# A list-scheduled attention and MLP kernel on one core: new order biases and planner costs, no instruction changed

## The chip, the cores and the metric

The kernel runs on one core of a Trainium2 chip. The metric is the device time of one execution in microseconds (us). The engines are TensorE (PE, with its weight loads shown as PEld), VectorE (DVE), ScalarE (ACT), GpSimd (POOL) and SyncE (SP). POOL and SP also issue the DMA transfers, each from its own queue, in order.

## The reference

```python
# attention: q, k, v are (8 batches, 8 heads, 576 positions, 64)
scores = q @ k.T / sqrt(64)
rel = i - j
mask_plain = (rel >= 0) & (rel < 32)                      # heads 0 to 3
mask_dil = (rel >= 0) & (rel < 128) & (rel % 4 == 0)      # heads 4 to 7
attn = softmax(where(mask, scores, -1e9)) @ v
x = attn.transpose(0, 2, 1, 3).reshape(4608, 512)
# MLP with a gated activation
h = x @ w_in                                              # 512 -> 2048
g = h * sigmoid(beta * h)
out = g @ w_out                                           # 2048 -> 512
```

## The kernel before, in words

The 4608 tokens are cut into 9 tiles of 512, and the work has two strands that are woven together. One is the MLP of a tile: for each of 16 blocks of the 2048 hidden columns `slot_h` issues four matmuls of 512 columns (L888), a tanh on ACT (L897) and the gate on DVE (L902); then `block_cols` multiplies with w_out, 16 matmuls of 512 columns for each 128 tokens (L923), evacuates on ACT (L938) or DVE (L940), and SP stores the rows (L943). The other is the attention of a batch (0 to 7), 576 tokens each. While the MLP of tile t is on PE, attention t + 1 is to be computed.

One attention has these parts, named by the lines that show in the profile:

- Loads. For batches 0 to 2 POOL loads q, k and v in bfloat16 straight into staging tiles (L395), and PE transposes q and k (L470 for the dilated heads, L480 for the plain ones), with copies out of PSUM at L244. From batch 3 on, POOL's loads write q and k as bfloat16 into scratch in DRAM (`s`), and SP reads them back with DMA transposes (L461) into dk and dq (dilated) and kT and qT (plain). Such a list of loads starts with a tiny POOL copy, `pace` (L1002). For batch 3 it waits for a gate of tile 1, and from batch 4 on for the transposed attention output xT of batch b - 2, both halves of it.
- V. vd is the dilated heads' V, vt the tail of it and vp the plain heads' V. vp has overlapping windows, so 32 rows are copied once more after its load: the halo copy, at L244 as `vp<-vp`, on DVE or POOL as the planner chooses. dkt is a copy of the last dilated keys, by `mixed` (L244), and qt the last queries.
- Scores on PE (L684 dilated, L653 its tail, L748 plain for batches 0 to 2 and L712 plain from 3 on, 24 at once), the exponential on ACT (L620), the mask on DVE or POOL (L624, tiles ptd, ptt and pt), the product with V on PE (L789 dilated, L774 tail, L805 plain), and the normalisation on DVE (L639, L640, into xdm, xdt and xsp).
- The way back. For batches 0 and 1 PE transposes the outputs (L842, L857, L827) into xT. From batch 2 on SP stores them to scratch `x` (L507, L515, L520) and reads them back by DMA transposes into xT (L534), two for a batch: xT0 and xT1.

Nothing of this order is written out by hand. Every piece is recorded as an `Op` in the class `Plan`: with the engines that it may run on and a cost in ns for each, the ops that it depends on, a due value `vt` and a bias, looked up in the table `NUDGE` by the op's number. `Plan.run` then does a list scheduling with these costs: for each engine it takes, among the ops that can start earliest (start plus bias, within the slack `NEAR`), the one with the smallest due value. The order that comes out is the order in which each engine's instructions are emitted, and an engine works strictly in that order, waiting on semaphores. `LAP` (L52) lets the planner start the next op on ACT or DVE 105 or 80 ns before the last one ends, if that one costs over 250 ns (L149). If the planner sees PE without work for more than 170 ns (300 early on) within the first 80 us, it emits a zero matmul (`filler`, L1036, 256 columns) into the hole. So a changed cost or bias can move any instruction of any queue.

The lines where the planner's costs stand: `mixed` at L582, the mask at L625, the halo copy in `direct_vp` at L417.

```python
picks = []
for e, c in near.items():
    first = min(s + o.bias for s, o, _ in c)
    s, o, d = min((x for x in c if x[0] + x[1].bias <= first + self.NEAR[e]), key=lambda x: (x[1].vt, x[0]))
    picks.append((s, o.vt, e, o, d))
```

Of the kernel before, what the change touches and what calls it, by code (L numbers as in the profile page):

```python
# [10 lines left out]
ACT = mybir.ActivationFunctionType  # L11
# [28 lines left out]
class Plan:  # L40
# [3 lines left out]

    CAPS = {"h": 3, "p": 4, "o": 2, "z": 4, "a": 8, "s": 5, "w": 6}
    SWITCH = 95
    NUDGE = {4: 900, 12: 900, 97: 400, 99: 150, 165: -900, 173: 150, 241: 60, 247: 400, 250: 900,
        268: -60, 285: 900, 299: -400, 309: 60, 312: -150, 362: 150, 405: 900, 424: -150, 496: 60,
        522: -900, 539: 150, 541: 900, 547: 150, 576: -400, 583: -400, 647: -150, 667: 900,
        675: -400, 717: -900, 796: -900, 808: 400}  # L50
    LAT = {"PE": 210, "ACT": 45, "DVE": 45, "POOL": 60, "SP": 0}
    LAP = {"PE": 0, "ACT": 105, "DVE": 80, "POOL": 0, "SP": 0}  # L52
    NEAR = {"PE": 40, "ACT": 60, "DVE": 60, "POOL": 60, "SP": 0}

    def __init__(self, banks):
# [2 lines left out]
    def op(self, engs, fn, deps=(), vt=0.0, acquire=None, group=None, dma=0, lat=None, halves=False, sbuf=False):  # L58
        acquire = acquire if acquire is None or isinstance(acquire, list) else [acquire]
        o = Op(engs, fn, deps, vt, acquire, group or acquire, dma, lat, halves, sbuf)  # L60
        o.bias = self.NUDGE.get(len(self.ops), 0)
        self.ops.append(o)
        return o

    def run(self, filler=None, filler_until=0.0):
        free = {"PE": 1100.0, "ACT": 1300.0, "DVE": 1000.0, "POOL": 1300.0, "SP": 1300.0}
# [22 lines left out]
        def bank_at(gs, start):  # L89
            kind, more = gs[0].kind, len(gs)  # L90
            n = [x.release for x in ends if x.kind == kind and x.release > start]
            n_open = sum(1 for x in held.values() if x.kind == kind)
            if n_open + more > self.CAPS[kind]:
                return None
            over = n_open + len(n) - self.CAPS[kind] + more
            if over > 0:
                start = sorted(n)[over - 1]
            open_banks = {x.bank for x in held.values()}
            times = sorted(t for b, t in bank_free.items() if b not in open_banks)
            return max(start, times[more - 1]) if len(times) >= more else None  # L100

        while n_left:
            best = None
            near = {}
            for o in avail:
                base = o.ready
                at = {e: max([free[e], base] + [t for x, t in o.group.read.items() if x != e]
                             if o.group is not None and e != "PE" else [free[e], base]) for e, d in o.engs}
                if o.sbuf:
                    at = {e: max(t, port["DVE" if e == "POOL" else "POOL"]) for e, t in at.items()}  # L110
                fin = min(at[e] + d for e, d in o.engs)
                for e, d in o.engs:
                    start = at[e]
                    if start + d > fin + 100:
                        continue
                    if o.dma and len(lanes[e]) >= 8:
                        start = max(start, lanes[e][-8])
                    if o.acquire is not None:
                        start = bank_at(o.acquire, start)
                        if start is None:  # L120
                            continue
                    near.setdefault(e, []).append((start, o, d))
# [5 lines that stand above are left out]
            assert picks, "no work can start"  # L128
            s, _, e, o, d = min(picks, key=lambda x: (x[0], x[1]))
            if filler is not None and s <= filler_until and free["PE"] + (300 if free["PE"] < COLD else 170) < s:  # L130
                now = free["PE"]
                open_banks = {x.bank for x in held.values()}
                spare = [b for b, t in bank_free.items() if b not in open_banks and t <= now]
                if spare:
                    filler(max(spare, key=lambda b: -bank_free[b]))
                free["PE"] = now + (225 if now < COLD else 115)
                halves = False
                continue
            for g in o.acquire or ():
                open_banks = {x.bank for x in held.values()}  # L140
                g.bank = min((b for b, t in bank_free.items() if b not in open_banks and t <= s + 1e-6),
                             key=lambda b: -bank_free[b])
                held[id(g)] = g
                g.left = len(g.users)
            o.fn(e)
            if e == "PE" and o.halves != halves:
                halves = o.halves
                d += self.SWITCH
            free[e] = s + d - (self.LAP[e] if d > 250 else 0)  # L149
            if o.sbuf:  # L150
                port[e] = s + d
            o.start, o.end = s, s + d + self.LAT[e]
            if o.group is not None and e != "PE":
                o.group.read[e] = o.end
            if o.dma:
                at = max(dma_free[e], s + d + 900)
                other = max(dma_free.values()) - at
                dma_free[e] = at + o.dma + max(0.0, min(o.dma, other))
                o.end = dma_free[e] + (o.lat or 1100)
                lanes[e].append(o.end)  # L160
            avail.remove(o)
            n_left -= 1
            for x in o.next:
                x.waits -= 1
                x.ready = max(x.ready, o.end)
                if not x.waits:
                    avail.append(x)
            for g in list(held.values()):
                if o in g.users:
                    g.left -= 1  # L170
                    if not g.left:
                        del held[id(g)]
                        g.release = max(u.end for u in g.users)
                        bank_free[g.bank] = g.release
                        ends.append(g)
            ends[:] = [g for g in ends if g.release > s - 5000]
# [9 lines left out]
def kernel(  # L186
# [49 lines left out]
    plan = Plan(range(8))  # L236
# [6 lines left out]
    def copy(e, out, in_):  # L243
        (nc.scalar.copy if e == "ACT" else E[e].tensor_copy)(out=out, in_=in_)  # L244
# [293 lines left out]
    def attention(b, ld, names, vts):  # L538
# [40 lines left out]

        def mixed(e):  # L580
            copy(e, dkt[kv], dk[kv][:, :, :, CT - KTL:].rearrange("p r h k -> p h k r"))
        o = plan.op([("DVE", 360), ("POOL", 550), ("ACT", 500)], mixed,  # L582
                    (steps["KD0"] + steps["KD1"] if b < DIRECT else ready["D"][0:1]) + war(("dkt", kv)), vt_of["T"] - .01, sbuf=True)
        used(("dk", kv, 0), o)
        used(("dk", kv, 1), o)
# [2 lines left out]
        for c in range(2):  # L588
            def padded(e, c=c):
# [3 lines left out]
            o = plan.op([("DVE", 250), ("POOL", 500), ("ACT", 290)], padded,  # L593
                        (steps["QD0"] + steps["QD1"] if b < DIRECT else ready["D"][1:]) + [fill1] + war(("qt", kv)),
                        vt_of["T"] - .01, sbuf=True)
# [10 lines left out]
        def spread(e):  # L606
            copy(e, vd[kv][:, :, :, 0:D], vd16_of[b])
        o = plan.op([("POOL", 1100), ("DVE", 620), ("ACT", 1030)], spread,
                    [ld["vd"][0], (fill3, fill4)[kv]] + war(("vd", kv)), vt, sbuf=True)
# [7 lines left out]
        def exp_and_mask(key, sop, g, vt, n, sc, w, m, tiles):  # L617

            def expo(e):
                nc.scalar.activation(out=w(), in_=sc(), func=ACT.Exp, scale=SCALE)  # L620
            ex = plan.op([act(n)], expo, [sop, fill2] + war(*tiles), vt - .005, group=g)
            if b >= ADDED or key == ("T",):
                def mask(e):
                    E[e].tensor_tensor(out=w(), in0=w(), in1=m(), op=ALU.mult)  # L624
                ex = plan.op([("POOL", 170 + 2.2 * n), ("DVE", 160 + .53 * n)], mask,  # L625
                             [ex] + [mask_tail if key == ("T",) else mask_ops["D" if key[0] in (2, 3) else "n"]],
                             vt, sbuf=True)
            wrote(*tiles)
            sdone[key] = ex
# [324 lines left out]
    for n, (c0, c1) in enumerate(((0, 512), (512, 1024), (1024, 2048))):  # L954
        o = load("POOL", (w_in_bf[:, :, c0:c1], moe_w_in[:, c0:c1].rearrange("(c p) d -> p c d", p=P)),
                 [], -7.3 + .01 * n, (c1 - c0) * 2, .41)
        for fb in range(c0 // P, c1 // P):
            w_in_ld[fb] = o
    for n in range(2):
        o = load("POOL", (w_out_bf[:, 8 * n:8 * n + 8, :],  # L960
                          moe_w_out[n * 8 * P:(n + 1) * 8 * P, :].rearrange("(c p) d -> p c d", p=P)),
                 [], -7.2 + .01 * n, 2048, .41)
# [107 lines left out]
```

## Time and profile before

| what | value |
| --- | --- |
| runs | 307.88, 305.89 and 303.32 us |
| median | 305.89 us |
| the profiled execution | 307.88 us, its span 306.1 us |
| PE busy in the span | 297.0 us, 97% |
| DVE, ACT, POOL busy | 190.8, 169.1 and 83.9 us |
| zero matmuls (L1036) | 61, 10.1 us busy |
| mean clock of PE | 1.0 in every slice but two (0.8) |
| DMA | 41.98 MB moved, mean 137 GB/s |

All times below are counted from the start of the span. A timeline row has the start, the length, the engine, the line, the operation with its tiles, and in brackets the idle time of the engine just before it and what ended that. Busy times of PE contain matmuls that overlap, so they can add up to more than the stretch that they fill.

### The profile page before, as it was taken

The numbers are of one execution on the slowest core, as the hardware profiler recorded it, in microseconds if no ns is written. First come the engines' busy times: TensorE is split into PE (matmuls) and PEld (weight loads), VectorE is DVE, ScalarE is ACT, GpSimd is POOL, SyncE is SP. The second block draws the span as 40 slices with busy tenths as digits, with TensorE's granted clock in tenths as the row PEclk, the third lists the DMA queues.
The fourth block names the chain that finished last, engine by engine and source line by source line (L and its number), as shares of the span: only waits on it lengthen the run. The fifth ranks groups of instructions, "written<-read, shape, count | busy, mean of one in ns | idle before, by whom it ended". The sixth has DMA issues, their size and how long they took to land.

```text
span 306.1 us, 6067 instructions
## 1 busy us (share of the span) xinstructions
PE 297.0 (97%) x2338; PEld 150.2 (49%) x2338; DVE 190.8 (62%) x429; ACT 169.1 (55%) x306; POOL 83.9 (27%) x121
## 2 busy tenths in 40 slices
PE   7999999999799999999999999999999999999996
PEld 5765455554354444544545454445444444444444
DVE  4668887799647846974678778656862534334300
ACT  3878932787334747754476657454744544455411
POOL 8997333681018005600632009100000000000000
PEclk9999999999889999999999999999999999999999
DMA  7999999699949999999699969995025000100122
GB/s 164 181 208 202 206 178 231 82 144 166 207 118 177 169 162 185 195 144 238 129 184 155 181 153 138 178 219 152 36 75 112 34 34 35 36 34 34 41 98 69
DMA packets 111248, 41.98 MB, mean 137 GB/s; under 512 B 87620, under 2 KB 104596, under 8 KB 111220
## 3 DMA queue, kind: packets, MB, share of 16 engines
q0 software_dynamic: 60336, 18.58, 58.8%
q1 hardware_dynamic: 50740, 22.95, 37.4%
q8 instruction: 18, 0.29, 0.4%
q14 instruction: 10, 0.08, 0.1%
q10 hardware_dynamic: 144, 0.07, 0.1%
HBM read 37.76 MB, written 18.87 MB: 185 GB/s over the span
## 4 chain that ended last, share of the span: by engine, by line
PE 83%; DMA 8%; DVE 4%; POOL 2%; ACT 1%; issue 1%; ACTq 0%; DVEq 0%; POOLq 0%
PE bank L923 38%; PE bank L888 36%; DMA vp<-in_v_dram 6%; DMA st<-in_q_dram 2%; PE bank L805 2%; DVE pt L624 1%; PE bank L1036 1%; PE bank L789 1%; PE bank L712 1%; POOL s L395 1%; DVE xdm L640 1%; PE bank L684 1%; PE bank L470 1%; PE bank L774 1%; DVE g L902 1%
## 5 line engine op out<-in xcount | busy, mean ns | idle before, releaser
L923 PE MATMUL bank<-w_out_bf,g 128*128 128x512 bf16 (+2 forms) x608 | 142.4, 370 | 0.0
L897 ACT ACTIVATE tnh<-bank,beta_half 128x512 bf16<-128x512 f32 x144 | 98.5, 689 | 74.8 <-PE bank L888 71.2
L902 DVE SCALAR_TENSOR_TENSOR g<-tnh,bank 128x512 bf16<-128x512 bf16 x144 | 97.5, 685 | 67.7 <-ACT tnh L897 66.9
L888 PE MATMUL bank<-xT,w_in_bf 128*128 128x512 bf16 (+2 forms) x584 | 138.7, 376 | 0.0
L888 PEld LDWEIGHTS <-w_in_bf 128*128 128x128 bf16 x584 | 55.3, 98 | 61.5 <-issue 1.1
L923 PEld LDWEIGHTS <-g 128*128 128x128 bf16 x608 | 55.4, 98 | 57.4 <-issue 1.0
L938 ACT ACTIVATE osb<-bank 128x512 f32<-128x512 f32 (+1 forms) x30 | 17.2, 576 | 28.2 <-PE bank L923 28.1
L620 ACT ACTIVATE pt<-bank 128x384 bf16<-128x384 f32 (+1 forms) x54 | 20.2, 469 | 7.6 <-PE bank L712 6.4
L620 ACT ACTIVATE ptd<-bank 128x512 bf16<-128x512 f32 x32 | 17.0, 605 | 6.9 <-PE bank L684 6.8
L624 DVE TENSOR_TENSOR pt<-pt,mask_n 128x384 bf16<-128x384 bf16 (+1 forms) x42 | 16.4, 415 | 5.4 <-ACT pt L620 5.1
L640 DVE TENSOR_TENSOR xsp<-bank,rcp 96x384 bf16<-96x384 f32 x32 | 17.7, 554 | 1.1
L1002 POOL COPY pace<-xT 1x2 bf16<-1x2 bf16 x4 | 0.7, 176 | 57.8 <-DMA xT<-x 57.8
L395 POOL DMA_DIRECT2D vp<-in_v_dram x9 | 15.2, 1695 | 0.4 <-DVE rcp L639 0.4
L639 DVE RECIPROCAL rcp<-bank 128x4 f32<-128x4 f32 (+2 forms) x72 | 12.8, 177 | 3.6 <-PE bank L789 2.9
L940 DVE TENSOR_SCALAR osb<-bank 128x512 f32<-128x512 f32 (+1 forms) x8 | 5.3, 658 | 14.8 <-PE bank L923 14.7
L395 POOL DMA_DIRECT2D vt<-in_v_dram x16 | 14.4, 1032 | 0.0
L640 DVE TENSOR_TENSOR xdm<-bank,rcp 128x256 bf16<-128x256 f32 x32 | 13.6, 425 | 1.1
L395 POOL DMA_DIRECT2D s<-in_q_dram x10 | 13.5, 1349 | 0.0
L624 DVE TENSOR_TENSOR ptd<-ptd,mask_d 128x512 bf16<-128x512 bf16 x27 | 10.9, 421 | 3.0 <-ACT ptd L620 2.4
L805 PEld LDWEIGHTS <-pt 128*128 128x128 bf16 x192 | 9.1, 97 | 6.0 <-DVE pt L624 1.1
L395 POOL DMA_DIRECT2D s<-in_k_dram x10 | 11.0, 1103 | 1.5 <-issue 1.1
L1036 PE MATMUL bank<-zero 128*128 128x256 bf16 x61 | 10.1, 303 | 1.1 <-DVE warm L303 1.1
(112 smaller groups left out, 179.6 us busy)
## 6 DMA issues: line engine op xcount, KB each, us to landing
out_dram<-osb SPq DMA_DIRECT2D x35, 256.0 KB, 2.6
s<-in_k_dram POOLq DMA_DIRECT2D x10, 288.0 KB, 5.9
s<-in_q_dram POOLq DMA_DIRECT2D x10, 288.0 KB, 8.8
w_out_bf<-in_moe_w_out_dram POOLq DMA_DIRECT2D x2, 1024.0 KB, 16.5
vp<-in_v_dram POOLq DMA_DIRECT2D x7, 288.0 KB, 17.5
st<-in_q_dram POOLq DMA_DIRECT2D x6, 288.0 KB, 11.1
x<-xsp SPq DMA_DIRECT2D x12, 144.0 KB, 6.9
st<-in_k_dram POOLq DMA_DIRECT2D x5, 288.0 KB, 13.4
```

The lines of the kernel that those rows point to most:

```text
L395: {"POOL": nc.gpsimd, "SP": nc.sync}[queue].dma_start(out=out, in_=in_)
L620: nc.scalar.activation(out=w(), in_=sc(), func=ACT.Exp, scale=SCALE)
L624: E[e].tensor_tensor(out=w(), in0=w(), in1=m(), op=ALU.mult)
L639: nc.vector.reciprocal(out=r, in_=p[..., D])
L640: nc.vector.tensor_tensor(out=dst, in0=p[..., 0:D], in1=r.unsqueeze(len(p.shape) - 1).to_broadcast(list(p.shape[:-1]) + [D]), op=ALU.mult)
L805: nc.tensor.matmul(pv[:, a, h2, :], lhsT=lhs, rhs=vp[kv][:, (2 * x + h2) * NI + 3 * j + a, 0:D + 1], start=True, stop=True)
L888: nc.tensor.matmul(bank(g)[:, a:z], lhsT=w_in_bf[:, kt, fb * P:(fb + 1) * P], rhs=xT[:, kt, xo + a:xo + z], start=(i == 0 and kt == kts[0] ...
L897: nc.scalar.activation(out=th[:, 0:n], in_=bank(g)[:, 0:n], func=ACT.Tanh, scale=beta_half[:, fb:fb + 1])
L902: nc.vector.scalar_tensor_tensor(out=g_t[t % 2][:, fb, c0:c0 + n], in0=th[:, 0:n], scalar=1.0, in1=bank(g)[:, 0:n], op0=ALU.add, op1=ALU.mult)
L923: nc.tensor.matmul(bank(g)[:, lo:hi], lhsT=g_t[t % 2][:, fb, tb * P:(tb + 1) * P], rhs=w_out_bf[:, fb, lo:hi], start=(fb == 0), stop=(fb = ...
L938: nc.scalar.mul(out=ob[:, lo:hi], in_=bank(g)[:, lo:hi], mul=0.5)
L1036: nc.tensor.matmul(BANKS[b][:, 0:256], lhsT=zero[:, 0:P], rhs=zero[:], start=True, stop=True)
```

## The change

Four edits, all in what the planner knows; the code that issues instructions stays.

1. `NUDGE`, the table of biases by op number, is replaced by another one.
2. `LAP` is removed: an engine counts as free only when the cost of its last op has passed.
3. The planner's cost for `mixed` on DVE goes from 360 to 450 ns.
4. The planner's cost for a mask on DVE goes from 160 + 0.53 n to 160 + 0.8 n ns, n being the elements of a row.

```diff
-    NUDGE = {4: 900, 12: 900, 97: 400, 99: 150, 165: -900, 173: 150, 241: 60, 247: 400, 250: 900,
-        268: -60, 285: 900, 299: -400, 309: 60, 312: -150, 362: 150, 405: 900, 424: -150, 496: 60,
-        522: -900, 539: 150, 541: 900, 547: 150, 576: -400, 583: -400, 647: -150, 667: 900,
-        675: -400, 717: -900, 796: -900, 808: 400}
+    NUDGE = {9: -400, 35: 400, 78: -150, 90: 150, 103: -900, 156: -900, 164: -60, 191: -60, 208: 150,
+        220: 900, 247: -400, 251: 60, 266: -150, 268: -150, 270: -150, 326: 900, 376: 400,
+        397: 900, 420: 900, 432: -900, 490: 900, 525: 150, 545: 60, 554: 900, 562: -60, 571: 60,
+        574: 150, 1103: -400, 1113: 400}
     LAT = {"PE": 210, "ACT": 45, "DVE": 45, "POOL": 60, "SP": 0}
-    LAP = {"PE": 0, "ACT": 105, "DVE": 80, "POOL": 0, "SP": 0}
...
-            free[e] = s + d - (self.LAP[e] if d > 250 else 0)
+            free[e] = s + d
...
-        o = plan.op([("DVE", 360), ("POOL", 550), ("ACT", 500)], mixed,
+        o = plan.op([("DVE", 450), ("POOL", 550), ("ACT", 500)], mixed,
...
-                ex = plan.op([("POOL", 170 + 2.2 * n), ("DVE", 160 + .53 * n)], mask,
+                ex = plan.op([("POOL", 170 + 2.2 * n), ("DVE", 160 + .8 * n)], mask,
```

What comes out of the planner differs in these places (line numbers as before; the same instructions otherwise):

- Zero matmuls: 67 for 61. Between 36 and 45 us of the profile, where 17 stood, 6 stand. Eight now stand within tile 0's L888 matmuls (after 8 of a dense run), where none did.
- Attention 0: half of the dilated K transposes follow those of q; both halves of the dilated scores come together after the plain K transposes; dkt is copied by DVE, and was by ACT.
- Attention 3: vp is loaded before plain q, and was after it; its halo copy is on POOL ahead of the tail mask, and was on DVE ahead of the dilated masks. On SP's queue qT's transpose stands before the store of batch 2's first plain output, and stood after it.
- Attention 4: vd is loaded early and vp last, and vd was last. The halo copy stays on DVE ahead of the four dilated masks; the copies of vd and dkt come earlier, between gates. On SP's queue the transposes xT0 and xT1 of batch 3 follow qT, and stood before and after kT.
- Tiles 2 and 3: L888 and L923 are interleaved otherwise.
- From batch 6 on the two orders nearly agree.

## The prediction

> **What bounds the kernel now.** I read the engines' shares first, then the slices, the chain that ended last, and then only the places where TensorE (PE) isn't dense.
>
> ```profile
> PE 297.0 (97%) x2338; PEld 150.2 (49%) x2338; DVE 190.8 (62%) x429; ACT 169.1 (55%) x306; POOL 83.9 (27%) x121
> PE   7999999999799999999999999999999999999996
> PEclk9999999999889999999999999999999999999999
> DMA  7999999699949999999699969995025000100122
> PE 83%; DMA 8%; DVE 4%; POOL 2%; ACT 1%; issue 1%; ACTq 0%; DVEq 0%; POOLq 0%
> ```
>
> PE is the bound: 97% busy and 83% of the chain. One slice is thin, the eleventh (76.5 to 84.2 us), and the granted clock dips there and just after. But busy is not useful: L1036 puts zero matmuls into holes. So I priced every other PE instruction at its dense start-to-start time in this trace (216 ns for 512 columns, 29 to 30 ns for 65, 109 to 110 ns for a zero matmul) and added them up: 283.4 us of useful work, and the last matmul ends at 303.1. Hence 1.1 us pass before PE's first work, 18.6 are lost to fillers and waits, and 3.0 follow behind it. The running loss is 9.1 at 19 us (the dense w_in run begins), 9.1 at 27, 12.7 at 44.5, 13.2 at 76.7, 17.1 at 95, and 18.6 at the end. So there are three places: the prologue, 36 to 44.5, and 76.7 to 85.
>
> ```profile
> 0.00:19.30 19.30, 16.65 (x266) 11.76 (x267) 12.54 (x44) 12.68 (x29) 17.27 (x37) 1.00 1.18 179
> 36.40:44.50 8.10, 7.38 (x74) 4.27 (x71) 7.21 (x19) 4.40 (x12) 3.79 (x6) 1.00 1.79 183
> 76.70:85.20 8.50, 6.42 (x62) 3.47 (x62) 4.81 (x13) 3.48 (x7) 0.66 (x1) 0.83 1.14 187
> ```
>
> These are windows: length, then PE, PEld, DVE, ACT, POOL busy, and the granted clock (0.83 in the third). Its cause stands in the chain of waits (start, length, what):
>
> ```profile
> 61.89 18.43 DMA vp<-in_v_dram
> 80.31 0.02 issue
> 80.34 0.48 DVE vp L244
> 80.82 0.03 issue
> 80.85 0.44 DVE ptd L624
> 81.29 0.05 issue
> 81.33 0.30 PE bank L789 x4
> ```
>
> For attention 3 the plain heads' V (vp) is the last load of its list and lands at 80.3. VectorE (DVE) waits for it with the halo copy (L244), and the dilated masks (L624), which don't need vp, are queued behind that copy. PE stands 2.08 us for the first, and then runs at half clock until 84.7. The stall takes 2.2 us and the half clock 1.7 of 3.4: 3.9 together.
>
> **The change, part by part.** No instruction changes its form. Biases, two planner costs and the removed overlap only alter the order on each queue, the engine of a few copies, and the zero matmuls (61 become 67). So each moved stretch is walked.
>
> A. Prologue: the K copy dk for pair 1 comes later on DVE, and half of the K transposes come after q. By rows of this trace the first dilated scores start 0.9 us later (8.65 becomes 9.55), the first plain ones 0.7 (11.79 becomes 12.45), and the dense w_in run 0.8. I take +0.8; the bounds are -0.4 (the fewer K transposes ahead of q help) and +2.0 (two PSUM copies of 0.64 and 0.75 behind the late one fall on PE).
>
> B. Eight zero matmuls now stand inside tile 0's L888 run, which had none: 8 x 0.11 = +0.9 where PE has work waiting, 0 where it would have waited anyway. I take +0.9.
>
> C. From 36 to 45 us, 17 zero matmuls (17 x 0.11 = 1.9 us) become 6 (0.7), and the scores come earlier. Of the 3.6 us lost there 1.7 were waits; about 1.0 stays, since four DVE normalisations of 0.55 us each still pace the back transposes (L842). 3.6 becomes 1.7: -1.9. The bounds are -2.9 (only the 0.7 stays) and 0 (PE stands idle where fillers stood).
>
> ```profile
> 42.70 0.38 PE L842 MATMUL bank<-ident_b,xdm 128*128 128x128 bf16 x4 [0.66 <-DVE xdm L640]
> 42.92 0.82 PE L1036 MATMUL bank<-zero 128*128 128x256 bf16 x6
> 43.80 0.38 PE L842 MATMUL bank<-ident_b,xdm 128*128 128x128 bf16 x4
> 44.02 0.60 PE L1036 MATMUL bank<-zero 128*128 128x256 bf16 x4
> ```
>
> D. Attention 3's halo copy moves to GpSimd (POOL), and vp is loaded ahead of plain q (s_1_0). DVE then reaches the masks with nothing to wait for: -3.9 (bounds -4.0 and 0). On POOL the copy takes 1.24 us for 0.48 and the tail mask, 0.7, stands behind it. With vp landing near 75 (plain q's old place) both end near 77, and their reader L774 comes at 67.6 useful plus 14.2 lost, 81.8: PE's own work covers them. If vp landed at 80.3 all the same, they would end at 82.3, and 0.5 would show.
>
> E. What D gives meets what D's swap delays. Plain q now has vp's place in POOL's list and lands at about 80.3 instead of 74.4.
>
> ```profile
> 60.79 2.17 POOL L395 DMA_DIRECT2D s<-in_q_dram  x1
> 61.89 2.25 POOL L395 DMA_DIRECT2D vp<-in_v_dram  x1
> 75.84 3.92 SPq L461 DMA_TRANSPOSE qT<-s  x1
> 87.10 1.31 SPq L534 DMA_TRANSPOSE xT<-x  x1
> 90.70 0.18 POOL L1002 COPY pace<-xT 1x2 bf16<-1x2 bf16 x1 [11.09 <-DMA xT<-x]
> ```
>
> On SP's queue qT's transpose waits for it, and behind qT now stand two x stores and both xT transposes of attention 2 (before, qT had gone out at 75.84). PE without D's stall would reach the plain scores (L712) at 71.65 of useful work plus 18.3 - 0.2 - 3.9 of loss = 85.9; qT lands 4.8 to 6.6 us after its issue (rows of attentions 4 and 3), at 85.1 to 86.9, so this is about even. Then: stores issue at 84.6 and land 2.7 later, xT0 at 87.3, an out store, xT1 at 89.3, landing 3.6 later: 92.9 (before 90.65). PE reaches tile 2's L888 at 77.06 + 14.2 = 91.3. So +1.6; the bounds are 0 and 6.6 (qT takes the 10.5 us of dk and dq in a loaded queue, landing at 90.8: 4.9 of stall and 1.7 of half clock).
>
> F. The pace copy that starts attention 4's loads waits for this xT1, so they start 2.2 us later. Their vp is now the last in the list, and its halo copy is still on DVE, ahead of all four masks.
>
> ```profile
> 113.31 0.48 DVE L244 COPY vp<-vp 32x1280 bf16<-32x1280 bf16 x1 [2.12 <-DMA vp<-in_v_dram]
> 114.77 0.43 DVE L244 COPY vd<-st 128x1024 bf16<-128x1024 bf16 x1 [0.98 <-DMA st<-in_v_dram]
> 115.11 1.74 DVE L624 TENSOR_TENSOR ptd<-ptd,mask_d 128x512 bf16<-128x512 bf16 x4
> ```
>
> The same stall was in the trace already, but PE came to L789 only at 117.17. The last load landed 24.1 us after the pace copy here, 20.3 in attention 5, 26.5 in 6. After the change two xT transposes stand behind qT and leave this window, so I take the middle of 24.1 and 20.3, 22.2: vp at 115.1, the first mask ready 0.95 later, 116.0; PE is there at 98.85 + 15.8 = 114.7. +1.3; the bounds are 0 (20.3) and 4.9 (24.1: 3.2 and half clock).
>
> G. Likewise attention 5: attention 3's xT1 now stands behind qT of 4 and lands at about 121 (before 117.85), and it paces 5's loads. dq, 21.6 us after its pace, lands at 142.6, and PE wants the scores at 124.35 + 17.0 = 141.4.
>
> ```profile
> 143.86 0.62 PE L684 MATMUL bank<-dq,dk 64*128 64x128 bf16 x16
> ```
>
> Before, dq landed at 139.6, 4.3 us ahead of this row; that slack is all that PE can gain here. +1.0 (bounds 0 and 3.0). From attention 6 on the orders nearly agree, and dq (166.8) has 6 us in hand: 0.
>
> Sum: 0.8 + 0.9 - 1.9 - 3.9 + 1.6 + 1.3 + 1.0 = -0.2. Against the profiled execution, 307.9 (span 306.1 and 1.8 around it), that is **307.7**. The profiled execution is 2.0 above the median of 305.9, possibly by the very stall that D takes out, so I don't take those 2 us off as well.
>
> [...] The stall of 2.08 us was followed by 3.41 us at half clock. [...]
>
> **The rivals.**
>
> R1, slower: attention 4's halo copy becomes the stall that 3's was. If the list takes 26.5 us (row of attention 6), vp lands at 92.9 + 26.5 = 119.4, the first mask is ready at 120.3, and PE has waited since 114.7: 5.6 and 1.7 of half clock instead of F's 1.3, and then nothing in G: 307.7 - 1.3 - 1.0 + 7.3 = 312.7. For it: in attentions 3, 4 and 6 the last load took 24 to 26.5 us. Against: 5 and 7 took 20. It decides once the list takes over 23.0 us, for then the hole passes the 2.1 us that cost clock.
>
> R2, the full gain: plain q lands in its old time because the list moves as a whole, and E, F and G are 0: 307.7 - 3.9 = 303.8. For it: dk, dq and kT wait for other loads, and qT's issue was bound by SP's queue. Against: the last in the list landed 5.9 us behind the one before it.
>
> R3, the early part is worse: A at +2.0 and C at 0 make 307.7 + 1.2 + 1.9 = 310.8. For it: DVE is busy 7.21 of 8.10 us in C's window, and a reordering takes nothing from it. Against: 11 fillers fewer.
>
> **How the numbers follow.** Forecast 0.42, R2 0.17, R3 0.16, R1 0.25. A measurement of this kernel tells about 2% from no change (runs spread from 303.3 to 307.9), so faster means below 299.8 and slower above 312.0. The forecast is within; R2 passes below with C's and A's good bounds (0.07 of its 0.17), R3 above with 0.05 of its 0.16, R1 with 0.18 of its 0.25: faster 0.07, within 0.70, slower 0.23. Range: from R2 with half of C's good bound, 302.0, to R1 with half of A's bad one, 313.5. The forecast's own range is 305 to 310.
>
> **What would show it.** D: L789 of attention 3 starts without a wait and the clock stays 1.0 around 80 us. E: s_1_0 lands near 80 and the pace copy near 93. F: an idle time before L789 near 115 ended by a mask behind the halo copy. G: an idle time before L684 near 142. C: loss of some 1.7 us between 36 and 45. If plain q lands at 75, E to G fall, and R2 holds; if PE isn't idle before L789 at attention 4 but the end is above 310, R3 does.

## The result and the profile after

| | kernel before | changed kernel |
| --- | --- | --- |
| median of 20 runs | 305.26 us | 303.00 us |
| shortest and longest | 303.32, 307.88 | 302.69, 303.53 |
| ratio, 95% interval | | 0.993 (0.9917 to 0.9944) |
| profiled execution | 307.88, span 306.1 | 302.73, span 301.0 |

The change makes the kernel 0.7% faster, and the interval leaves out 1; the forecast said 307.7, on the other side of the median. The ratios leave out runs that are over 1.5% longer than the kernel's fastest one, while medians are of all runs, so a ratio can differ from that of the two medians. Two things strike the eye beside that. The profiled execution of before, from which the forecast was worked out, is the longest of its 20, and the runs of the changed kernel lie within 0.8 us of each other where those of before spread over 4.6.

The page of the changed kernel (its line numbers are one lower than before's):

```profile
PE 295.5 (98%) x2344; PEld 150.4 (50%) x2344; DVE 187.5 (62%) x424; ACT 172.2 (57%) x311; POOL 83.9 (28%) x121
PEclk9999999999999999999999999999999999999999
PE 94%; DVE 2%; ACT 1%; POOL 1%; issue 1%; POOLq 0%; ACTq 0%
```

No slice has a lowered clock, and the chain that ended last is 94% PE, with no DMA in it (before: 83%, and 8% DMA). The windows that answer to those shown of before (PE, PEld, DVE, ACT, POOL busy, then the granted clock, the busy share of the DMA engines and GB/s):

```profile
36.40:44.50 8.10, 7.83 (x73) 4.04 (x71) 6.20 (x19) 5.61 (x14) 2.42 (x4) 1.00 1.84 181
76.70:85.20 8.50, 8.50 (x84) 4.44 (x82) 6.73 (x19) 4.24 (x9) 0.70 (x2) 1.00 0.86 198
```

The third place is dense. In the first of the two, DVE is busy 6.20 us instead of 7.21: that second difference turned out to matter.

To see where time was won I took PE's own work at its dense start-to-start times again, and read when each execution has done the same share of it. The orders differ, so a row is good to about half a us. `b_again` is the kernel before once more, in another execution:

| share of PE's work | before, us | b_again, us | changed, us | changed less b_again |
| --- | --- | --- | --- | --- |
| 3.0% | 21.05 | 20.88 | 20.89 | 0.0 |
| 4.5% | 24.92 | 24.74 | 25.80 | +1.1 |
| 10.4% | 47.04 | 46.85 | 46.01 | -0.8 |
| 20.4% | 77.03 | 76.83 | 76.37 | -0.5 |
| 24.1% | 91.96 | 88.35 | 87.85 | -0.5 |
| 38.9% | 133.57 | 130.39 | 129.30 | -1.1 |
| 53.8% | 176.24 | 172.66 | 171.15 | -1.5 |
| last matmul's end | 303.09 | 299.50 | 297.94 | -1.6 |

Against the execution that I had, 3.5 us come from the stall near 81 us (the rows of 20.4 and 24.1%). Against that of b_again nothing comes from there. The medians differ by 2.3 us, these two executions only by 1.5: b_again's was the shortest of its 12 runs, so the rest of the gain presumably lies in waits that it did not have.

### The profile page after: what moved, and what is told of

It is laid out like the page before. It is cut to its first block, busy times and chain, and to the rows that moved or that the text cites. A ratio compares the mean times of both kernels' runs of the same rounds, so it can differ in the third digit from the quotient of the medians.

```text
span 301.0 us, 6071 instructions
## 1 busy us (share of the span) xinstructions
PE 295.5 (98%) x2344; PEld 150.4 (50%) x2344; DVE 187.5 (62%) x424; ACT 172.2 (57%) x311; POOL 83.9 (28%) x121
## 4 chain that ended last, share of the span: by engine, by line
PE 94%; DVE 2%; ACT 1%; POOL 1%; issue 1%; POOLq 0%; ACTq 0%
PE bank L922 41%; PE bank L887 40%; PE bank L804 2%; PE bank L1035 2%; PE bank L683 1%; PE bank L788 1%; PE bank L711 1%; PE bank L469 1%; PE bank L747 1%; PE bank L479 1%; ACT ptd L619 1%; PE bank L773 1%; DVE xdm L639 1%; PE bank L673 1%; DVE ptd L623 1%
## 5 line engine op out<-in xcount | busy, mean ns | idle before, releaser
L922 PE MATMUL bank<-w_out_bf,g 128*128 128x512 bf16 (+2 forms) x608 | 140.0, 368 | 0.0
L887 PE MATMUL bank<-xT,w_in_bf 128*128 128x512 bf16 (+1 forms) x584 | 137.0, 376 | 0.0
L922 PEld LDWEIGHTS <-g 128*128 128x128 bf16 x608 | 54.5, 98 | 55.7
L937 ACT ACTIVATE osb<-bank 128x512 f32<-128x512 f32 (+1 forms) x35 | 20.6, 589 | 31.3 <-PE bank L922 30.7
L623 DVE TENSOR_TENSOR pt<-pt,mask_n 128x384 bf16<-128x384 bf16 (+1 forms) x41 | 14.8, 391 | 5.7 <-ACT pt L619 5.5
L623 DVE TENSOR_TENSOR ptd<-ptd,mask_d 128x512 bf16<-128x512 bf16 x27 | 12.0, 465 | 3.6 <-ACT ptd L619 3.0
L394 POOL DMA_DIRECT2D vt<-in_v_dram x16 | 13.3, 993 | 0.0
L1035 PE MATMUL bank<-zero 128*128 128x256 bf16 x67 | 11.6, 310 | 1.3 <-DVE warm L302 1.1
L804 PE MATMUL bank<-vp,pt 128*128 128x65 bf16 x192 | 9.8, 193 | 0.0
```

The source lines that it names most:

```text
L394: {"POOL": nc.gpsimd, "SP": nc.sync}[queue].dma_start(out=out, in_=in_)
L804: nc.tensor.matmul(pv[:, a, h2, :], lhsT=lhs, rhs=vp[kv][:, (2 * x + h2) * NI + 3 * j + a, 0:D + 1], start=True, stop=True)
L887: nc.tensor.matmul(bank(g)[:, a:z], lhsT=w_in_bf[:, kt, fb * P:(fb + 1) * P], rhs=xT[:, kt, xo + a:xo + z], start=(i == 0 and kt == kts[0] ...
L922: nc.tensor.matmul(bank(g)[:, lo:hi], lhsT=g_t[t % 2][:, fb, tb * P:(tb + 1) * P], rhs=w_out_bf[:, fb, lo:hi], start=(fb == 0), stop=(fb = ...
L937: nc.scalar.mul(out=ob[:, lo:hi], in_=bank(g)[:, lo:hi], mul=0.5)
L1035: nc.tensor.matmul(BANKS[b][:, 0:256], lhsT=zero[:, 0:P], rhs=zero[:], start=True, stop=True)
```

## The experiments

To move one instruction and nothing else, these kernels keep the planner's list (`seq`), move single entries of it, and issue the result; line numbers shift by up to some ten, by one in b_again. `at(n)` is the place of op n in the list. Names with b_ start from the kernel before, names with a_ from the changed one. `n` is the op's number: 531 is attention 3's halo copy, 530 its vp load, 525 its plain q load, 585 the second transpose of its output (xT1), 664 attention 4's kT transpose.

```python
def move(n, ahead_of, e=None):
    o, was = seq.pop(at(n))
    seq.insert(at(ahead_of), (o, e or was))
```

All ratios are to the kernel before, timed on the same chip in the same rounds; its median there lay between 304.8 and 305.6. There were four such groups of rounds, on three chips, so medians of different groups compare only to within those 0.8 us.

| kernel | median, us | shortest, longest | ratio, 95% interval |
| --- | --- | --- | --- |
| b_again | 305.60 | 304.27, 307.73 | 1.0013 (0.9984 to 1.0042) |
| b_halo | 305.19 | 303.19, 308.57 | 1.0004 (0.9975 to 1.0033) |
| b_vp | 305.32 | 303.90, 307.89 | 1.0010 (0.9977 to 1.0044) |
| b_vp_halo | 304.95 | 303.38, 308.92 | 0.9986 (0.9961 to 1.0012) |
| b_xt | 304.22 | 302.88, 309.17 | 0.9982 (0.9954 to 1.0011) |
| b_halo_xt | 304.23 | 303.10, 305.86 | 0.9974 (0.9952 to 0.9997) |
| b_nofill17 | 304.69 | 303.69, 306.33 | 0.9986 (0.9957 to 1.0015) |
| b_mask | 304.34 | 302.63, 309.16 | 0.9965 (0.9933 to 0.9998) |
| b_all3 | 303.56 | 302.36, 306.73 | 0.9962 (0.9930 to 0.9995) |
| oldbias_newcost | 303.45 | 302.18, 306.61 | 0.9952 (0.9917 to 0.9987) |
| newbias_oldcost | 312.44 | 311.08, 313.62 | 1.0238 (1.0198 to 1.0278) |
| a_undo3 | 302.87 | 302.52, 304.25 | 0.9923 (0.9891 to 0.9956) |
| a_nofill8 | 302.75 | 302.48, 302.95 | 0.9919 (0.9891 to 0.9948) |
| a_mask | 302.22 | 301.73, 303.64 | 0.9917 (0.9886 to 0.9948) |
| a_mask_nofill8 | 301.79 | 301.37, 302.92 | 0.9886 (0.9849 to 0.9923) |
| a_best | 301.67 | 301.35, 302.14 | 0.9878 (0.9843 to 0.9914) |

### The stall of attention 3

b_again changes nothing that is issued.

> The kernel before once more, nothing changed. Its profiled execution was the longest of 20 (307.88 us, median 305.26), so a second profile shows what a usual execution looks like. If the stall of attention 3 is what varies, this profile has a shorter idle time before L789 near 81 us (under 2 us), and no half clock behind it, and the span is shorter by as much, about 303.5 us. If the stall is the same (2.1 us and 3.4 us at half clock), the spread of the runs comes from elsewhere. Ratio to before 1.000.

Its profiled execution took 304.27 us. vp landed at 77.75, not 80.3, and PE did not wait for the masks at all; the clock stayed 1.0. So the 2.08 us and the half clock belong to the long execution. That a usual one lacks them is less sure, since this was the shortest run of its 12; but the profiles of b_nofill17 (304.45, near its median), b_xt and b_mask, which leave vp and the halo copy as they were, show no wait for these masks either.

b_halo:

```diff
+ move(531, 547, 'POOL')    # the halo copy, ahead of the tail mask
```

> The kernel before with one copy moved: attention 3's halo copy goes from DVE (ahead of the dilated masks) to POOL (ahead of the tail mask). Loads as before. Theory of the stall: the idle time before L789 near 81 goes, vp still lands near 80, the copy on POOL ends near 81.6 and the tail mask at 82.3, before L774 needs it or 0.5 us late; the median falls from 305.3 by 2 to 3 us, to 302.3 to 303.3. Rival, the early part: the gain of the changed kernel comes from fewer zero matmuls between 36 and 45 us, and a usual execution hardly has the stall: within 0.5 us of before.

Nothing: 1.0004, runs still up to 308.6. The interval leaves room for a gain of 0.8 us at most, not for the 2 to 3 that were expected. The stall as the gain falls, for the median at least, and so far the rival "early part" stands.

b_vp and b_vp_halo:

```diff
+ move(530, 525)            # vp ahead of plain q
+ move(531, 547, 'POOL')    # b_vp_halo only
```

> The kernel before with one load moved: attention 3's vp is loaded ahead of plain q; the halo copy stays on DVE. Theory of the stall: vp lands at 73 to 75, so the copy is over long before the masks, and the stall goes; plain q lands near 77 and qT near 81, before L712 (about 85): 302.3 to 303.3. Rival, the delay that the forecast charged: plain q lands near 80, qT near 86, the second transpose of attention 2's output near 93, and the pace copy behind it; 304.5 to 306.

> The kernel before with both moves: vp ahead of plain q, the halo copy on POOL. Theory of the stall: no more than either alone, 302.3 to 303.3, since one is enough. Rival, the two add up: vp first takes the copy's wait, POOL takes its 0.5 us from DVE; 0.5 us or more below the better of the two.

Neither differs from before. The profiles are worth more than the times. In b_vp's, a long execution of 307.76, plain q landed at 80.40 (vp at 75.23), qT went out then, and the pace copy came at 91.33, for 80.3 and about 93 in the forecast. In b_vp_halo's, a shorter one of 303.96, they were 79.46 and 90.11 (b_again, without the swap: pace copy at 87.54). So in the order of before the swap does delay the pace copy, by some 2.6 to 3.8 us against b_again, and the median doesn't show it. And b_vp's shows the next stall, in the row of tile 3's first w_in matmuls (start, length, engine, what, and the idle time before it):

```profile
117.99 1.24 PE L898 MATMUL bank<-xT,w_in_bf 128*128 128x512 bf16 x5 [1.98 <-DMA xT<-x]
```

PE waits 1.98 us for xT1 of attention 3. b_again has the same wait with 0.39 us. The execution of the forecast does not show it, since PE was 3.9 us late there when it came to it.

### Tile 3's wait for xT1

b_xt and b_halo_xt:

```diff
+ move(585, 664)            # xT1 of attention 3 ahead of kT of attention 4, on SP
+ move(531, 547, 'POOL')    # b_halo_xt only
```

> The kernel before with two moves: attention 3's halo copy on POOL, and on SP's queue the second transpose of attention 3's output (xT1) ahead of attention 4's kT, which stood before it. New theory, two stalls in turn: in the kernel before either the masks of attention 3 wait for vp, or tile 3's first w_in matmuls wait for xT1 near 115 us (0.5 to 2.1 us in the profiles so far); mending one alone only hands its time to the other. With both mended the median falls from 305.4 to about 304.0 and the longest run stays below 305.5. Rival, the early part alone: the changed kernel's gain is the 1 us between 36 and 47 us and its narrow spread has another cause; then this stays within 0.5 us of before with runs up to 308.

> The kernel before with xT1 of attention 3 ahead of attention 4's kT on SP's queue, and nothing else. Two stalls in turn: the wait of tile 3's w_in matmuls goes, that of attention 3's masks stays and is now paid in full in each run that has it; 304.5 to 305, runs up to 308. Rival, tile 3's wait alone is what costs: 304.0, and a narrow spread.

Both medians are 304.2, and in neither profile does tile 3 wait. With both moves the longest run is 305.9; with xT1 alone it is 309.2. That fits two stalls of which now one and now the other is paid, but doesn't show it: b_all3 below has both moves too, and a run of 306.7. The interval of b_xt alone includes 1, so only the pair is shown to gain, 0.03 to 0.5%. For b_xt 304.5 or more was expected; as the medians are equal, what the halo copy adds to xT1 is not shown.

In the changed kernel SP's queue is no better in this: xT1 stands behind qT. But tile 3's first w_in matmuls come later in PE's order, behind the plain scores of attention 4, and start without a wait:

```profile
118.22 0.69 PE L711 MATMUL bank<-qT,kT 64*128 64x96 bf16 x24
118.84 1.04 PE L922 MATMUL bank<-w_out_bf,g 128*128 128x512 bf16 x4
119.72 2.75 PE L887 MATMUL bank<-xT,w_in_bf 128*128 128x512 bf16 x12
```

xT1 lands at 115.19 there, 4.5 us before it is used.

### Zero matmuls

b_nofill17 leaves out the last 17 zero matmuls of before, a_nofill8 the 8 within tile 0's w_in matmuls of the changed kernel.

> The kernel before without its last 17 zero matmuls (36 to 45 us); they compute nothing that is used. If PE had work behind them, 1.9 us less: 303.5. If they only fill waits for DVE's normalisations, the holes stay as idle time: 305.4, and the clock stays 1.0 because no hole is over 1 us.

> The changed kernel without the 8 zero matmuls within tile 0's w_in matmuls; they compute nothing that is used. As the forecast's part B has it, PE has work behind them and they cost 0.9 us: 302.1 against 303.0 for the changed kernel. Rival: what follows waits for a copy or an exponential in any case, so the 0.9 us comes back as a wait by 47 us: 303.0.

b_nofill17: no difference that can be told. Most of the holes remain, as idle time ahead of the two back transposes:

```profile
43.04 0.38 PE L851 MATMUL bank<-ident_b,xdm 128*128 128x128 bf16 x4 [1.06 <-DVE xdm L649]
...
44.14 0.38 PE L851 MATMUL bank<-ident_b,xdm 128*128 128x128 bf16 x4 [0.71 <-DVE xdm L649]
```

Between two fixed PE instructions around the place (the plain scores at 36.8 and the w_out matmul at 44.5 us of b_again) its profile takes 7.39 us, b_again's 7.72: 0.33 us, not 1.9.

a_nofill8 is 0.25 us below the changed kernel, not 0.9. The medians are of different rounds, but the profiles agree: from 21 to 60 us the same PE work takes 0.23 to 0.24 us less in each of the three kernels without these eight (a_nofill8, a_mask_nofill8, a_best). The place shows a wait for the gate on DVE instead, 0.48 us of idle time in all three. Of the 1.9 and 0.9 us of fillers 0.33 and 0.25 came back: these mostly stood where PE would wait.

### Undoing attention 3's part in the changed kernel

a_undo3:

```diff
+ move(525, 530)            # plain q ahead of vp again
+ move(531, 538, 'DVE')     # the halo copy ahead of the dilated masks again
```

> The changed kernel with attention 3 put back as before: plain q ahead of vp, the halo copy on DVE ahead of the dilated masks. All else as changed. Theory: what the changed kernel has over the one before is the later place of tile 3's w_in matmuls (slack for xT1) and the 1 us before 47 us; its list for attention 3 starts 1.5 us earlier, so vp lands near 77 and the masks (80 us) hardly wait: 303.0 to 303.6, a few runs 1 to 2 us longer. Rival, the forecast's part D: without the swap the stall of up to 3.9 us is back: 304.5 to 306 with runs up to 308.

302.87 for the changed kernel's 303.00: the swap and the copy's place, which the forecast spent most of its pages on, are worth nothing in the median that can be told. Its longest run, the profiled one of 304.25, shows a halo stall at another attention:

```profile
172.03 0.30 PE L799 MATMUL bank<-vd,ptd 128*128 128x65 bf16 x4 [1.25 <-DVE ptd L634]
```

### One half of the change without the other

newbias_oldcost takes the new bias table with the old costs and overlap; oldbias_newcost the reverse.

> One part of the change alone: the new table of biases, with the planner's old costs and overlap. The biases were numbers for ops in a plan with the new costs; theory: they don't carry over, so this is another order with its own stalls, 304 to 309, above the changed kernel. Rival, the biases are the gain: 303.0.

> The other part alone: the new costs and no overlap in the planner, with the old table of biases. Theory: as for the other half, an order of its own, 304 to 309. Rival, truer costs are the gain, with any biases: 303 to 304.

The new biases on the old costs are 2.4% slower than before, above the 304 to 309 us that were expected, and the profile shows the largest cost: the wait of tile 3 at 5.54 us, and the clock at a mean of 0.69 in the 11 us from 123 on.

```profile
129.85 2.72 PE L888 MATMUL bank<-xT,w_in_bf 128*128 128x512 bf16 x6 [5.54 <-DMA xT<-x]
```

The new costs with the old biases reach 303.45, the rival's 303 to 304, but with runs up to 306.6. By the ratio this is 0.5 of the 0.7%, with an interval that includes both 0.1 and 0.8. Its profiled execution, 305.30, shows a halo stall once more, at attention 5: PE waits 1.74 us for the first dilated mask and then runs 3.41 us at half clock. So the costs alone bring a gain, the biases alone a loss, and only both together the narrow spread.

### The masks of DVE and POOL

What was open after this: 304.2 with the two stalls mended against 303.0. The stretch from 36 to 44 us differs in DVE's busy time, and b_again shows its cause. First DVE, then POOL, the plain heads' masks of attention 1:

```profile
37.54 1.42 DVE L625 TENSOR_TENSOR pt<-pt,mask_n 128x288 bf16<-128x288 bf16 x2 [0.27 <-ACT pt L621]
...
40.41 0.95 DVE L625 TENSOR_TENSOR pt<-pt,mask_n 128x288 bf16<-128x288 bf16 x2
```

```profile
37.82 0.75 POOL L625 TENSOR_TENSOR pt<-pt,mask_n 128x288 bf16<-128x288 bf16 x1
```

The execution of the forecast has the same collision:

```profile
37.72 1.47 DVE L624 TENSOR_TENSOR pt<-pt,mask_n 128x288 bf16<-128x288 bf16 x2 [0.27 <-ACT pt L620]
38.20 0.83 POOL L624 TENSOR_TENSOR pt<-pt,mask_n 128x288 bf16<-128x288 bf16 x1
```

Two such masks take 0.52 us where DVE is alone. Beside POOL's they take 1.42, and later 0.95. Everything behind them on DVE, the four normalisations first, is 1.0 us later than without (b_mask, below), and PE's back transposes wait for these. The changed kernel has one plain mask on POOL in this stretch (at 40.23) instead of two, and no DVE mask beside it. The list of differences ahead of the prediction doesn't name this one. b_mask puts POOL's two masks on DVE:

```diff
+ move(250, 171, 'DVE')
+ move(248, 276, 'DVE')     # behind the last of the four normalisations
```

> The kernel before with two masks of attention 1's plain heads on DVE instead of POOL, one in its place and one behind the last of the four normalisations near 43 us. In most profiles of the kernel before, POOL's mask starts at 37.8 to 38.4 us beside two DVE masks, and these take 1.20 and 0.73 us for 0.30; the normalisations and the back transposes on PE come 1.1 us later. In one profile (with xT1 moved) POOL came 0.3 us later, nothing was stretched, and PE lost 1.1 us less. Theory of the collision: no stretch, PE loses 0.8 to 1.1 us less before 47 us in every execution; median 304.3 to 304.8 from 305.3, stalls behind it as before. Rival, the zero matmuls and the normalisations set that stretch anyway: no change before 47 us, 305.3.

```profile
37.73 0.61 DVE L635 TENSOR_TENSOR pt<-pt,mask_n 128x288 bf16<-128x288 bf16 x2 [0.27 <-ACT pt L631]
...
40.03 0.52 DVE L635 TENSOR_TENSOR pt<-pt,mask_n 128x288 bf16<-128x288 bf16 x2
```

DVE does two masks more and is done sooner. Between the two fixed PE instructions b_mask takes 6.71 us and b_all3 (below) 6.72. Of the executions with before's masks and fillers, five take 7.72 or 7.73 and b_halo's 7.55. b_xt's takes 6.71 too: there POOL's masks happened to come later, at 38.68 and 40.19, and stretched no DVE mask. So the collision costs 1.0 us here. At 10.4% of PE's work this execution stands at 46.04 us, the changed kernel at 46.01, b_again at 46.85: the collision is as large as the net gain of the early part. It isn't the same sum, since the changed kernel also pays 0.9 us of zero matmuls there (B below). The median falls by 0.45 us beside before's in the same rounds (0.9965, 0.9933 to 0.9998).

b_all3 is b_mask and b_halo_xt together.

> The kernel before with all three: these two masks on DVE, attention 3's halo copy on POOL, xT1 of attention 3 ahead of kT of attention 4 on SP's queue. Theory: these three are the gain of the changed kernel; 304.2 (the latter two) less 0.8: 303.2 to 303.6, no run above 305. Rival, the later place of tile 3's w_in matmuls on PE brings something that these don't: 304 or more.

303.56, at the upper end of what was expected, and beside before's 304.79 in the same rounds: 0.4 of the change's 0.7% is rebuilt from three moves, in a kernel that has none of the change. The interval (0.9930 to 0.9995) reaches from the whole gain to hardly any, so what the rest is stays open. Two of the 12 runs, 305.8 and 306.7, are above the 305 that I expected as the longest. The profile, of a run of 304.07, has a wait of 0.54 us at 79.8: two dilated masks of 0.42 us took 1.44 on DVE beside POOL's halo copy, and 0.88 beside its tail mask. So the moved halo copy makes a collision of its own.

The changed kernel has such a collision too, at 61 us: DVE, then POOL, then PE.

```profile
61.39 1.55 DVE L623 TENSOR_TENSOR ptd<-ptd,mask_d 128x512 bf16<-128x512 bf16 x1 [0.55 <-ACT ptd L619]
62.86 1.23 DVE L623 TENSOR_TENSOR ptt<-ptt,mask_t 96x256 bf16<-96x256 bf16 x1
```

```profile
61.51 2.42 POOL L623 TENSOR_TENSOR ptd<-ptd,mask_d 128x512 bf16<-128x512 bf16 x1
```

```profile
64.69 0.28 PE L788 MATMUL bank<-vd,ptd 128*128 128x65 bf16 x4 [0.73 <-DVE xdm L639]
```

The two masks take 0.42 and 0.28 us alone. a_mask moves POOL's mask (397) to DVE, a_mask_nofill8 also leaves out the 8 zero matmuls, a_best also puts the halo copies of attentions 4 to 6 on POOL:

```diff
+ move(397, 399, 'DVE')
+ for n in (671, 811, 951):             # a_best only
+     i = at(n)
+     seq[i] = (seq[i][0], 'POOL')
```

> The changed kernel with one dilated mask of attention 2 moved from POOL to DVE, ahead of the one that ran beside it. In the changed kernel's profile two DVE masks beside that POOL mask took 1.55 and 1.23 us for 0.42 and 0.28, the POOL mask 2.42 for 1.37, and PE then waited 0.9 us for a normalisation queued behind them (near 64 us). Theory, DVE and POOL hold each other up when both read two inputs: the stretch goes, and 0.5 to 0.9 us with it: 302.1 to 302.5. Rival: the wait moves on to the next transfer (the loads of attention 3), nothing is gained: 303.0.

> The changed kernel with one dilated mask of attention 2 on DVE and without the 8 zero matmuls in tile 0's w_in matmuls (they compute nothing that is used). Each alone gave 302.2 and 302.75. If they add up: 301.9 to 302.0. If the early time is taken back by a wait for attention 3's loads: 302.2.

> The same with the halo copies of attentions 4, 5 and 6 on POOL, in their places. In profiles of variants the masks behind the halo copy made PE wait 0.35 us at 140 and 170 us, once 1.4, once 1.9. If the copy off DVE ends that: 301.2 to 301.7. Rival, the POOL copy runs beside the masks and stretches them: 302.0 or more.

302.22, 301.79 and 301.67. The first is the theory's value, though its interval overlaps that of the changed kernel. The profiles are clearer: between the same PE instructions at about 60 and 70 us the three without the collision take 9.27 or 9.28 us, the three with it (the changed kernel, a_nofill8, a_undo3) 10.16 to 10.29. In a_mask's profile DVE does four masks in 1.77 us:

```profile
60.01 1.77 DVE L633 TENSOR_TENSOR ptd<-ptd,mask_d 128x512 bf16<-128x512 bf16 x4
61.69 0.28 DVE L633 TENSOR_TENSOR ptt<-ptt,mask_t 96x256 bf16<-96x256 bf16 x1
```

The second is 0.1 us below what adding up would give. The third is within 301.2 to 301.7 as expected, but only 0.1 below a_mask_nofill8, too little to tell. Its rival came in part: beside two of the halo copies on POOL a DVE mask took 1.33 and 1.35 us for 0.42, and yet PE did not wait there. a_best is 1.2% below before (0.9843 to 0.9914). Its longest run, 302.14, is shorter than the shortest of the changed kernel, 302.69, though those are of other rounds.

## Why the prediction was wrong, point by point

- A, the prologue (+0.8): 0. At 3.0% of the work b_again and the changed kernel stand at 20.9 us; over all profiles this mark spreads over 0.8 us, with no difference between the orders. The late dk copy delays the scores as walked (9.55), but the holes that it makes were filled with waits anyway.
- B, eight zero matmuls (+0.9): their 0.9 us are there (25.80 against 24.92), but only 0.25 of it comes back when they are left out, for a gate is late next.
- C, 36 to 45 us (-1.9): the size is right, in part by luck: from 7.4 to 10.4% of the work before loses 4.1 us beyond that work and the changed kernel 2.3. The reason given, fewer fillers, carries little of it: without any filler there before gains nothing that the median can tell, and 0.33 us in the profile. The four normalisations did pace the place, as the forecast said, but 1.0 of the 1.8 us came from two masks stretched by POOL, which stand in the forecast's own trace and which it doesn't count. What made the other 0.8 is not shown; some of it may be fillers.
- D, the halo stall (-3.9): about right for the execution that it was read from (3.5 us), and it is gone there; only the half clock lasted to 85.7 in that trace, not 84.7. For the median it is worth nothing that can be told (b_halo 1.0004, a_undo3 302.87 beside 303.00). The forecast named the doubt, that the profiled execution's excess might be this stall, and then used it to keep the higher number.
- E (+1.6): **this is the step that failed first.** "Plain q now has vp's place in POOL's list and lands at about 80.3" is right in the order of before (80.40 in b_vp, 79.46 in b_vp_halo) and wrong in the changed one, where it landed at 76.66. Its list began 1.6 us earlier, since the gate of tile 1 that it waits for ran earlier, and was through in 21.9 us instead of 24. The five profiles of the changed order with the swap took 21.6 to 22.9 us, b_vp 24.0 and b_vp_halo 23.2, b_again without it 21.6; what shortens the list in the changed order is not shown. And xT1, which had stood behind an x store that waited for the stalled normalisation, now stands ahead of it: it landed at 87.25, not 92.9. The rows of the queue, of the halo copy and of the next pace copy:

```profile
59.22 1.73 POOL L394 DMA_DIRECT2D vp<-in_v_dram  x1
60.39 2.18 POOL L394 DMA_DIRECT2D s<-in_q_dram  x1
...
75.49 1.24 POOL L243 COPY vp<-vp 32x1280 bf16<-32x1280 bf16 x1
...
87.30 0.17 POOL L1001 COPY pace<-xT 1x2 bf16<-1x2 bf16 x1 [7.71 <-DMA xT<-x]
```

- F (+1.3) and G (+1.0): 0, because both hung on E's late pace copy. F's length was even at its upper bound, 24.2 us from the pace copy to vp:

```profile
111.49 0.48 DVE L243 COPY vp<-vp 32x1280 bf16<-32x1280 bf16 x1 [2.66 <-DMA vp<-in_v_dram]
112.00 1.62 DVE L623 TENSOR_TENSOR ptd<-ptd,mask_d 128x512 bf16<-128x512 bf16 x4
```

  PE came to L788 at 113.08, some 0.65 us after the first mask was ready. In G, dq landed at 135.29 and was wanted at 138.67. (The 20.3 us that F took for attention 5 is vp's landing; the last load of that list landed after 21.3. By that, F would have been 0.5 larger. And G's own numbers, 142.6 and 141.4, give 1.2, not 1.0.)
- Of the 4.7 us charged in A, E, F and G none was paid; that is nearly the distance between the sum of -0.2 and the -5.1 between the two profiled executions. Rival R2, the full gain with 303.8, described the changed profile best, yet its reason (attention 3's stall) isn't what the medians show; that it came so near the median is luck. The low end of the range was mis-summed: R2 with half of C's good bound is 303.8 - 0.5 = 303.3, not 302.0, and with C's and A's good bounds 301.6, which does not pass 299.8.
- What the forecast lacked: the wait of tile 3 for xT1, which the long execution hid, and the collision of masks. Shown are the collision (b_mask, and the profiles around a_mask) and that the two moves of b_halo_xt gain together. Open is the rest of the change's gain, about half of it by b_all3. That the later place of tile 3's matmuls is what keeps the changed kernel's spread narrow is argued from the rows; it wasn't tried alone.

## What to carry to other kernels

Before a stall of one profile is priced, look where that execution lies among the run times: where runs spread, the profile shows one of several stalls, and one that is paid can hide the next (here the longest of 20 had 2.08 us of wait for attention 3's masks and none for xT1, b_again 0.39 us for xT1 and none for the masks). A wait that ends in a DMA is worked out from when the list before it starts, and that start moves with the same change (here by 1.6 us). Where rows of one form take two or three times their usual length (here 1.42 us for 0.52 and 1.55 for 0.42, each beside a mask of POOL), look what ran beside them before counting instructions.

## What the runs showed of the hardware

- In these traces DVE and POOL held each other up in masks: in the changed kernel 0.42 became 1.55 us on DVE and 1.37 (before, at 63.95) became 2.42 on POOL when they ran together. It was one-sided in b_again: POOL's 128x288 mask took 0.75 us beside two DVE masks, which took 1.42 for 0.52, and one in the changed kernel, at 40.23 with no DVE mask beside it, 0.73. In the changed kernel the first DVE mask started 0.12 us ahead of POOL's, the second ended 0.16 us after it (64.09 against 63.93), and the three took 2.70 us together, more than the 2.07 of their lengths alone. That both engines must read two inputs for it, as the theory of a_mask has it, is not shown: in b_all3 and a_best a DVE mask of 0.42 us took 1.33 to 1.44 beside POOL's halo copy, which reads one tile.
- A hole of 2.08 us in PE was followed by 3.41 us at half clock in the execution of the forecast, and one of 1.74 us likewise in oldbias_newcost; holes of 1.98 us (b_vp), 1.25 us (a_undo3), 1.06 and 0.71 us (b_nofill17) left the clock at 1.0. So the length of the hole alone doesn't decide it, and R1's 2.1 us is no limit that these runs show. What decides it is not shown.
- Lists of eight loads took 17.9 to 26.5 us from their pace copy to the last landing. Attention 3's alone took 21.0 to 24.0 in before and the b_ kernels that keep its order of these loads. Such a spread is larger than most margins here.
